# A fused attention and mixer kernel: the token blocks of two pair groups taken whole, and five turns of one group moved from TensorE to DMA

**Chip, cores, metric.** One core of a Trainium2 chip (8 cores on two dies; this program uses one). The metric is the device time of one execution in microseconds (us), the median of several runs.

## The reference

Sigmoid attention for 8 batches x 12 heads (448 tokens, head size 64), then a mixer layer: a token MLP (448 to 256 to 448) on the transposed x, an addition, and a channel MLP (768 to 1536 to 768), another addition.

```python
scores = scale * np.matmul(q, k.transpose(0, 1, 3, 2)) - np.log(S)
attn = 1.0 / (1.0 + np.exp(-scores))
x = np.matmul(attn, v)                      # heads are then laid side by side: (8, 448, 768)
h = np.maximum(x.transpose(0, 2, 1) @ w_tok1, 0.0) @ w_tok2
u = x + h.transpose(0, 2, 1)
h2 = np.maximum(u @ w_ch1, 0.0) @ w_ch2
out = u + h2
```

## The kernel before

Batches 0 and 1 run alone ("A", "B"); batches 2 to 7 are three *pair groups* 1, 2, 3. While the channel matmuls of one group run on TensorE (PE), the attention of the next group is mixed into them, so that ScalarE (ACT), which makes the sigmoids, works beside PE. A Python program plans this: it keeps a rough clock for each engine, and writes the next piece of the main stream (channels) or of the second stream (attention and token MLP) by what is ready. The order on the chip is fixed by that plan. A small edit can therefore reorder everything after it.

One pair of heads gives seven *rounds* of scores (four matmuls and one sigmoid each), then the values, whose result xT has x transposed. The *back* turns it to the tokens' layout. Two ways exist:

```python
def back_by_dma(g, i):                       # one DMA turn on the SP queue
    c = slice(128 * (i % 3), 128 * (i % 3) + 128)
    nc.sync.dma_start_transpose(
        out=x_of(g, i // 3)[:, :, c], in_=xT[(g, i)].rearrange("d b s -> d (b s)")
    )
    did("sp", 1.4, [("xT", g, i)], [("x", g, i)], DMAT)

def back(g, i, at):                          # seven PE transposes and one DVE copy
    ...
    for t in range(J):
        nc.tensor.transpose(out=ps[:, t, :], in_=x[:, 128 * t : 128 * t + 128], identity=ident[:, :])
    nc.vector.tensor_copy(out=x_of(g, i // 3)[:, :, c], in_=ps[:, :, :])
    ...
```

After a group's last pair comes its *token block*: two token matmul groups (first layer, second half) and seven pieces of the second layer. Each of the seven makes u on VectorE (DVE), an fp16 copy u16 on ACT, and a DMA turn of it into uT. All seven turns must land before the group's channel matmuls can start. I call that moment the *hand-over*; there are three, one for each pair group.

```python
u16 = pa.tile([128, D], FP16, tag="attn", bufs=ATTN, name=f"u16_{g}_{t}")   # ATTN = 8
copy("act", u16[:, :], u_of(g, t)[:, :])
...
nc.sync.dma_start_transpose(out=uTs[g][:, :, 128 * t : 128 * t + 128], in_=u16[:, :])
```

The fp16 copies share eight buffers with the sigmoid results. The plan of the second stream, before:

```python
for u, needs, f, made in attention_stays(PAIRS[3:]):   # entries of two rounds each
    if g != u and not late and (g == "B" or out[g][1]):
        g = after_unit[g]
        out[g] = ([], [])
    if late:                                            # the token block: 9 pieces
        out[g][1].append((needs, f))                    # two rounds of the next group first
        take = TAKE[0] if len(late) == 9 else len(late) # TAKE = (5,): 5 pieces, then
        out[g][1].extend(late[:take])                   # two more rounds, then 4 pieces
        late = late[take:]
    else:
        out[g][0].append((needs, f))
    ...
```

Of the kernel before, what the change touches and what calls it, by code (L numbers as in the profile page):

```python
# [21 lines left out]
def kernel(  # L22
# [69 lines left out]
    DIRECT = (3, 0)  # L92
    FROM = (10, 44)
    LATE, MIX = 8, 46
    TAKE = (5,)
    BACK_BY_DMA = [(3, i) for i in range(5)]
    KEYS = ((0, 3), (3, J))
    WARM = 9
    BANKS = ("m0", "m1", "m2", "m3")
# [406 lines left out]
    def tok1(g, half, tcb):  # L506
        x = x_of(g, half)
        ps = pair_bank(f"k1_{g}_{half}_{tcb}", [128, 2, 512])
        for b in range(2):
            for n in range(4):  # L510
                nc.tensor.matmul(  # L511
                    out=ps[:, b, 0:DH],
                    lhsT=w_tok1_of(b, n, tcb),
                    rhs=x[:, n + 3 * b, :],
                    start=(n == 0),
                    stop=(n == 3),
                )
        h = pa.tile([128, 2, DH], FP16, tag="tmp", bufs=4, name=f"h1T_{g}_{half}_{tcb}")
        h1T[(g, half, tcb)] = h
        relu(engine_of(g), h[:, :, :], ps[:, :, 0:DH])  # L520
        pe(1.3, [("x", g, 3 * half + i) for i in range(3)] + [rot["at"]], ["pe"])
        evac(engine_of(g), D, ["pe"], [("h1", g, half, tcb), rot["at"]])
# [8 lines left out]
    def h1_keys(g):  # L531
        if g in SINGLE:
            return [("h1", g, i) for i in range(KD)]
        return [("h1", g, half, t) for half in range(2) for t in range(2)]

    def tok2_pair(g, t):
        ps = pair_bank(f"yn_{g}_{t}", [128, 2, 512])
        for half in range(2):
            for tcb in range(2):
                for b in (0, 1) if t == MIXED else (t // 4,):  # L540
                    c = 64 + 128 * t if t < MIXED else 128 * (t - MIXED)
                    w = w_tok2_of(tcb, c, 128)
                    o = ps[:, half, 0:DH]
                    if t == MIXED:
                        w = w_tok2_of(tcb, S if b == 0 else 64, 64)
                        o = ps[64 * b : 64 * b + 64, half, 0:DH]
                    nc.tensor.matmul(  # L547
                        out=o,
                        lhsT=w,
                        rhs=h1T[(g, half, tcb)][:, b, :],  # L550
                        start=(tcb == 0),
                        stop=(tcb == 1),
                    )
        pe(0.65, h1_keys(g) + [rot["at"]], ["pe"], "col" if t == MIXED else "full")
        for half in range(2):
            dve(0.47, ["pe"], [("u", g, t), rot["at"]])
            nc.vector.tensor_tensor(  # L557
                out=u_of(g, t)[:, DH * half : DH * half + DH],
                in0=x_of(g, half)[:, t, :],
                in1=ps[:, half, 0:DH],  # L560
                op=ADD,
            )
        u16 = pa.tile([128, D], FP16, tag="attn", bufs=ATTN, name=f"u16_{g}_{t}")
        copy("act", u16[:, :], u_of(g, t)[:, :])
        evac("act", D, [("u", g, t)], [("u16", g, t)])
        did("sp", 1.4, [("u16", g, t)], [("uT", g, t)], DMAU)
        state["turned"] = g
        if g not in uTs:
            uTs[g] = pa.tile([128, NDB, 2 * S], FP16, tag="uT", bufs=1, name=f"uT_{g}")
        nc.sync.dma_start_transpose(  # L570
            out=uTs[g][:, :, 128 * t : 128 * t + 128], in_=u16[:, :]
        )

    def tok2_single(g, n, half):

        at = either()
        ps = bank(f"yn_{g}_{n}_{half}", [128, DH], at=at)
        c = 64 - OFF[g] + 128 * n
        for tcb in range(2):
            nc.tensor.matmul(  # L580
                out=ps[:, :],
                lhsT=w_tok2_of(tcb, c, 128),
                rhs=h1T[(g, tcb)][:, half, :],
                start=(tcb == 0),
                stop=(tcb == 1),
            )
        pe(0.33, h1_keys(g) + [f"m{at}"], ["pe"])
        t = n + (3 if g == "B" else 0)
        r = slice(0, 128)
        if t == MIXED:  # L590
            r = slice(0, 64) if g == "A" else slice(64, 128)
        dve(0.47, ["pe"], [("u", g, n), f"m{at}"])
        nc.vector.tensor_tensor(
            out=u_of(g, t)[r, DH * half : DH * half + DH],
            in0=x_of(g, 0)[r, n, half, :],
            in1=ps[r, :],
            op=ADD,
        )
# [516 lines left out]
    def turned_back(g, i):  # L1115

        keys = [("xT", g, i), "m2/m3" if g in SINGLE else "m3"]
        if g not in SINGLE and i % 3 == 0:
            if g == 1:
                keys.append(("u", "AB"[i // 3], 3))  # L1120
            else:
                keys.append(("uT", g - 1, LAST))
        if (g, i) in BACK_BY_DMA:
            del keys[1]
# [14 lines left out]
    def attention_stays(pairs):  # L1139


        out, due, made = [], [], None
        rounds = [(g, i, j) for g, i in pairs for j in range(J)]
        while rounds or due:
            ops, needs, made = [], ["two banks"], None
            if due:
                made = due.pop(0)
                ops.append(lambda at=made: value_stay(*at))
                needs.append(("attn", *made, J - 1))
                needs.append(("one", "value"))  # L1150
                needs += [("x", *ahead(*made, -1))]
            while rounds and len(ops) < 2:
                g, i, j = rounds.pop(0)
                ops.append(lambda at=(g, i, j): one(*at))
                needs += [("k", g, i), ("q", g, i)]
                if j == J - 1:
                    due.append((g, i))
            out.append((g, needs, lambda ops=ops: run(ops), made))
        return out

    def token_entries(g):

        def first(half, t):
            keys = ["one bank"] + [("x", g, 3 * half + i) for i in range(3)]
            return keys, lambda: tok1(g, half, t)

        def second(m):
            keys = [("h1", g, half, t) for half in range(2) for t in range(2)]
            if m >= 5:
                keys.append(("stored", g - 1, STORED[g - 1][m - 5]))  # L1170
            return ["one bank"] + keys, lambda: tok2_pair(g, ORDER[m])

        if g in SINGLE:
            return [], [
                (
                    h1_keys(g) + ["m2/m3", ("x", g, KD - 1)],
                    lambda n=n, half=half: tok2_single(g, n, half),
                )
                for n in range(4)
                for half in range(2)  # L1180
            ]
        return (
            [first(0, 0), first(0, 1)],
            [first(1, 0), first(1, 1)] + [second(m) for m in range(J)],
        )

    def side_stream():

        g, out, late = "B", {"B": ([], [])}, []
        for u, needs, f, made in attention_stays(PAIRS[3:]):  # L1190
            if g != u and not late and (g == "B" or out[g][1]):
                g = after_unit[g]
                out[g] = ([], [])
            if late:
                out[g][1].append((needs, f))
                take = TAKE[0] if len(late) == 9 else len(late)
                out[g][1].extend(late[:take])
                late = late[take:]
            else:
                out[g][0].append((needs, f))  # L1200
            if made and made[0] not in SINGLE and made[1] == NPAIR[made[0]] - 1:
                early, late = token_entries(made[0])
                for n, x in enumerate(early):
                    out[g][0].insert(len(out[g][0]) - 2 + n, x)
        out[g][1].extend(late)
        return out
# [172 lines left out]
    with tc.manual_schedule(engines=None):  # L1379
# [40 lines left out]
        load_pair(1, 1)  # L1420

        stream = side_stream()
        ahead_of_all = [(0.0, *x) for x in stream["B"][0]]
        first_attention(ahead_of_all)
# [144 lines left out]
        for m in range(16):  # L1569
            made = base["B"] + NCB  # L1570
# [42 lines left out]
```

## Time and profile before

| | before |
|---|---|
| median of its first three runs | 373.42 us (373.2 to 374.18) |
| span in the profile | 372.6 us, granted clock 0.988 |
| PE busy | 355.9 us, 96% of the span |
| ACT waits for landed turns (uT) | 7.3 us in 3 waits |
| PE waits for uT at the first hand-over | 2.25 us |

PE is the engine to watch: a change counts if it takes work off PE or closes a hole in it. The lines behind the table are in the prediction.

### The profile page before, as it was taken

To read this page: it belongs to the slowest core of one execution; us is meant where nothing else is said; L and a number is where in the kernel's file an instruction comes from. 1 tells how busy PE (TensorE), PEld (TensorE's weight loads), DVE (VectorE), ACT (ScalarE), POOL (GpSimd) and SP (SyncE) were. 2 spreads that over 40 slices of the span, in tenths; PEclk is the share of its full clock that TensorE was granted. 3 is DMA by queue.
4 is the path that set the end of the run, shared out by engine and by line. 5 is a ranking of instruction groups with operands and counts; after the bars stand their busy time and mean duration, and the time that the engine had idled before them with its cause. 6 is when DMAs were issued, how large, how long until landed. Compare 5 with 4: busy or idle time off the path is not lost.

```text
span 372.6 us, 7828 instructions
## 1 busy us (share of the span) xinstructions
PE 355.9 (96%) x3148; PEld 182.6 (49%) x3148; DVE 235.3 (63%) x440; ACT 195.6 (52%) x240; POOL 132.1 (35%) x213
## 2 busy tenths in 40 slices
PE   6899999999999999799999999899999999999994
PEld 2445545444444555344444555444445556455562
DVE  2267667668645578696643568765644678665862
ACT  2697365666655344367785654287777352243000
POOL 8983313465657510056666410055530000004000
PEclk9699999999999999999999999999999999999998
DMA  6999999889998928798998748798873057400143
GB/s 80 177 193 200 152 211 170 101 147 150 146 149 129 140 49 85 173 164 126 128 121 136 102 103 129 196 164 149 127 122 69 2 126 148 130 0 2 42 147 106
DMA packets 82082, 46.50 MB, mean 125 GB/s; under 512 B 56576, under 2 KB 78336, under 8 KB 82048
## 3 DMA queue, kind: packets, MB, share of 16 engines
q0 software_dynamic: 24576, 21.93, 40.5%
q1 hardware_dynamic: 56912, 22.72, 32.3%
q10 hardware_dynamic: 560, 1.38, 1.0%
q8 instruction: 24, 0.39, 0.4%
q14 instruction: 10, 0.08, 0.1%
HBM read 43.84 MB, written 11.01 MB: 147 GB/s over the span
## 4 chain that ended last, share of the span: by engine, by line
PE 80%; DMA 6%; ACT 6%; DVE 3%; issue 2%; POOL 2%; SPq 0%; ACTq 0%; POOLq 0%
PE x L741 11%; PE qk L422 8%; PE x L1004 7%; PE xa L440 7%; DMA uT<-u 5%; PE z L741 5%; PE k L511 4%; PE c_B L860 4%; PE c_A L860 4%; PE z L1004 3%; PE c_A L918 3%; PE d L1061 3%; PE y L741 2%; PE c_B L918 2%; PE yn L547 2%
## 5 line engine op out<-in xcount | busy, mean ns | idle before, releaser
L429 ACT ACTIVATE attn<-qk 128x896 f16<-128x896 f32 x126 | 109.6, 915 | 50.3 <-PE qk L422 49.9
L741 PEld LDWEIGHTS <-w 128*128 128x128 f16 x378 | 34.3, 98 | 43.1 <-issue 15.1
L422 PE MATMUL qk<-qT,kT 64*64 64x448 f16 x504 | 39.3, 361 | 1.6 <-ACT attn L429 0.8
L741 PE MATMUL x<-uT,w 128*128 128x448 f16 x162 | 37.9, 353 | 2.4 <-DMA uT<-u 2.2
L756 DVE COPY c<-x 128x448 f32<-128x448 f32 x42 | 26.1, 622 | 20.8 <-PE x L741 20.6
L761 DVE CUSTOM_DVE_ANT_0 h2T<-z,c 128x448 f16<-128x448 f32 x36 | 22.5, 624 | 18.5 <-PE z L741 16.3
L394 POOL COPY gate<-kT 1x2 f16<-1x2 f16 x16 | 3.5, 217 | 81.4 <-DMA kT<-pk 81.4
L218 ACT ACTIVATE u<-u 128x768 f16<-128x768 f32 x21 | 17.5, 842 | 24.7 <-DVE u L557 16.9
L246 POOL DMA_DIRECT2D k<-in_k_dram x36 | 21.4, 601 | 23.0 <-PE tk L351 13.2
L1016 DVE TENSOR_TENSOR u<-u,x 128x384 f32<-128x384 f32 x36 | 19.8, 552 | 14.1 <-PE x L1004 14.1
L1004 PEld LDWEIGHTS <-h2T 128*128 128x128 f16 x216 | 20.8, 98 | 15.3 <-issue 2.0
L440 PE MATMUL xa<-attn,v 64*64 64x448 f16 x504 | 27.3, 352 | 0.5 <-ACT attn L429 0.5
L429 ACT ACTIVATE attn_B<-qk_B 128x896 f16<-128x896 f32 x21 | 18.3, 914 | 14.3 <-PE qk_B L422 14.3
L741 PE MATMUL z<-s,w 128*128 128x448 f16 x108 | 24.3, 353 | 0.0
L422 PEld LDWEIGHTS <-kT 64*64 64x64 f16 x504 | 12.4, 104 | 23.0 <-issue 20.6
L557 DVE TENSOR_TENSOR u<-x_nat,yn 128x384 f32<-128x384 f16 x42 | 20.9, 549 | 3.3 <-PE yn L547 2.7
L246 POOL DMA_DIRECT2D v<-in_v_dram x36 | 22.2, 644 | 1.6 <-DMA k<-in_k_dram 1.3
L661 POOL TENSOR_TENSOR r<-h2T,h2T 128x512 f16<-128x512 f16 x1 | 1.2, 1153 | 60.5 <-ACT h2T L230 60.5
L429 ACT ACTIVATE attn_A<-qk_A 128x896 f16<-128x896 f32 x21 | 17.5, 923 | 9.3 <-PE qk_A L422 9.3
L338 POOL COPY pk<-k 128x896 f16<-128x896 f16 x17 | 15.9, 937 | 17.9 <-DMA k<-in_k_dram 17.6
L338 POOL COPY pq<-q 128x896 f16<-128x896 f16 x17 | 15.9, 936 | 17.1 <-DMA q<-in_q_dram 17.1
L246 POOL DMA_DIRECT2D q<-in_q_dram x36 | 21.8, 626 | 0.1
(137 smaller groups left out, 635.9 us busy)
## 6 DMA issues: line engine op xcount, KB each, us to landing
out_dram<-u SPq DMA_DIRECT2D x49, 192.0 KB, 2.9
k<-in_k_dram POOLq DMA_DIRECT2D x36, 112.0 KB, 3.0
q<-in_q_dram POOLq DMA_DIRECT2D x36, 112.0 KB, 4.1
v<-in_v_dram POOLq DMA_DIRECT2D x36, 112.0 KB, 4.3
w<-in_moe_w_ch_dram POOLq DMA_DIRECT2D x2, 1152.0 KB, 11.5
w<-in_moe_w_ch_dram POOLq DMA_DIRECT2D x1, 2304.0 KB, 22.7
out_dram<-u ACTq DMA_DIRECT2D x7, 192.0 KB, 3.2
q_A<-in_q_dram POOLq DMA_DIRECT2D x6, 112.0 KB, 4.4
```

Of the source, the lines that this page charges most:

```text
L246: nc.gpsimd.dma_start(out=t[64 * side : 64 * side + 64, :, :, :], in_=src[b, h + 2 * i : h + 2 * i + 2].rearrange("h (p j) e -> p h j e", ...
L338: nc.gpsimd.tensor_copy(out=m[:, :, :, :], in_=raws[(g, i, what)].rearrange("p h j e -> p j h e"))
L422: nc.tensor.matmul(out=ps[64 * b : 64 * b + 64, h, 0:S], lhsT=keys_of(g, i, j)[r, b, :], rhs=qT[(g, i)][r, :, b, :], start=True, stop=True,)
L429: nc.scalar.activation(out=at[:, :, :], in_=ps[:, :, 0:S], func=SIGMOID, bias=att_bias, scale=att_scale)
L440: nc.tensor.matmul(out=ps[b][64 * h : 64 * h + 64, :], lhsT=vf[r, h, j, :], rhs=attn[(g, i, j)][r, h, :], start=(j == 0), stop=(j == J - 1),)
L557: nc.vector.tensor_tensor(out=u_of(g, t)[:, DH * half : DH * half + DH], in0=x_of(g, half)[:, t, :], in1=ps[:, half, 0:DH], op=ADD,)
L741: nc.tensor.matmul(out=ps[:, :], lhsT=W(p, n, cb), rhs=A[p](n), start=(first and n == 0), skip_group_check=True, stop=(n == KD - 1),)
L756: nc.vector.tensor_copy(out=s[:, :], in_=bk[(cb, "x")][:, :])
L761: nc.vector._custom_dve(dve_ops.TENSOR_ADD_SAT, out=h[half][:, cb, S * b : S * b + S], in0=ps[:, :], in1=snap[(cb, n)][:, :], s0=BIG, s1=0.0,)
L860: nc.tensor.matmul(out=bk[cb][:, :], lhsT=w1[:, n, 128 * cb : 128 * cb + 128], rhs=uTs[g][:, n, OFF[g] : OFF[g] + S], start=(n == 0), stop ...
L1004: nc.tensor.matmul(out=ps[:, :], lhsT=A(p, n, kb), rhs=W(p, kb), start=(first and kb == 0), skip_group_check=True, stop=(kb == KC - 1),)
L1016: nc.vector.tensor_tensor(out=u, in0=u, in1=ps[:, :], op=ADD)
```

## The change

The token blocks of groups 1 and 2 are taken whole (nine pieces) before the next group's fifth and sixth round, so that fewer sigmoid results hold buffers meanwhile; and group 2's first five backs go through DMA as group 3's did already. The sixth back of each group stays on PE.

```diff
-    TAKE = (5,)
-    BACK_BY_DMA = [(3, i) for i in range(5)]
+    TAKE = {1: 9, 2: 9, 3: 9}
+    BACK_BY_DMA = [(g, i) for g in (2, 3) for i in range(5)]
@@ side_stream
-                take = TAKE[0] if len(late) == 9 else len(late)
+                take = TAKE.get(mixed) if len(late) == 9 else len(late)
@@
                 early, late = token_entries(made[0])
+                mixed = made[0]
```

## The prediction

> **What bounds the kernel now.** I read the page first: TensorE (PE) is busy for 96% of the span at almost full granted clock, and the slices show no stage in which it rests, apart from short dips. So a change can only help by taking work off PE or by closing one of those dips.
>
> ```profile
> span 372.6 us, 7828 instructions
> PE 355.9 (96%) x3148; PEld 182.6 (49%) x3148; DVE 235.3 (63%) x440; ACT 195.6 (52%) x240; POOL 132.1 (35%) x213
> ...
> PE   6899999999999999799999999899999999999994
> DMA  6999999889998928798998748798873057400143
> ```
>
> The "7" in the middle of the PE row is the hand-over from the single batches to pair group 1. The DMA row matters too: the 16 engines are 70 to 100% busy for most of the time in which group 2 is prepared (153 to 215 us). Next I took the chain of work that ended last, from 139.8 to 153.5 us. It leaves PE:
>
> ```profile
> 139.61 0.79 PE yn L547 x8
> ...
> 142.39 3.57 DMA uT<-u
> ...
> 146.07 0.76 ACT u L218
> ...
> 148.25 4.32 DMA uT<-u
> 152.56 0.25 issue
> 152.81 0.73 PE x L741 x3
> ```
>
> The token results u are copied to fp16 by ACT, turned by a DMA, and only then can the channel matmuls of the group start. One copy waits for an earlier turn (3.57 us), then a second turn follows (4.32 us). The timelines of ACT and of PE say what this costs:
>
> ```profile
> 146.07 1.64 ACT L218 ACTIVATE u<-u 128x768 f16<-128x768 f32 x2 [2.31 <-DMA uT<-u]
> ```
> ```profile
> 152.81 0.73 PE L741 MATMUL x<-uT,w 128*128 128x448 f16 x3 [2.25 <-DMA uT<-u]
> ```
>
> ACT stood 2.31 us because the fp16 copy had no free buffer, and PE then stood 2.25 us. The program explains the buffer: copies and sigmoid results share eight buffers. While two more rounds of the next group lie inside the block, six sigmoid results are alive and two buffers stay for the last copies. At the hand-over to group 2 the waits from 215 to 241 us are:
>
> ```profile
> ACT u L218 <- DMA uT<-u: 5.0, 2, 3.0
> ...
> PE x L741 <- DVE c L756: 0.8, 1, 0.8
> ...
> PE x L1004 <- DVE u L1016: 0.4, 1, 0.4
> ```
>
> Here ACT stands 5.0 us in two waits, but PE has output matmuls of the old group to do, and loses only 0.8 + 0.4 us.
>
> Last, the turns back. The windows of group 2 show PE full while five of its six turns of x (the backs) run on it:
>
> ```profile
> 180.42 0.73 PE L741 MATMUL x<-s,w 128*128 128x448 f16 x3
> 180.99 0.55 PE L486 MATMUL xb<-ident,xT 128*128 128x128 f16 x7
> 181.47 0.57 PE L422 MATMUL qk<-qT,kT 64*64 64x448 f16 x8
> ```
>
> **What the Trainium skill says.** "Perfetto Trace Analysis", Identifying Performance Opportunities, says that repeated bubbles can mean there is no space for the next tile. The trace agrees, as the three ACT waits on uT (7.3 us in all) show. "VectorE: DVE Perf Modes", The three transpose paths, puts a 128x128 transpose at 390 ns on TensorE and 1309 ns through DMA. So DMA is no faster as such. The trace agrees in direction: the DMA turn of group 3's x takes 4.6 us from issue to landing, seven PE transposes 0.55 us; what is bought is PE time, not latency. "DMA: Bandwidth & Descriptors", Issuing engines are not separate DMA queues, says that all queues end on the same 16 engines and interleave. That is the risk of this change, since the loads of q, k and v run then. The trace has both streams in one window, but one run cannot separate them.
>
> **The change part by part.**
>
> *Backs of group 2.* Five turns of seven transposes leave PE and five copies of 0.62 us leave DVE; five DMA turns of 1.22 us of issue are added to the SP queue. Per back on PE: above, from the start of the three matmuls before it to the scores after it, 181.47 - 180.42 = 1.05 us. Without a back, the same two things stand 0.66 us apart (160.41 to 161.07). So one back costs 0.39 us, five cost 5 x 0.39 = 1.95 us. PE is full there, so this is on the path. DVE is busy 27 to 89% in the ten-microsecond windows from 153 to 203 us and PE hardly waits for it: its 3.1 us count nothing. The added latency has room: the turn lands 4.6 us after issue (6.2 at most in group 3), and the next pair's result, which needs the same buffer, comes 10 us later.
>
> *Block of group 1, hand-over at 152.8.* With all nine pieces ahead of the next rounds, four sigmoid results are alive and four buffers are left for seven copies. The last piece then comes without the scores of two rounds (0.6 us of PE) and without the matmuls that filled the time until their banks were free: about 140 us instead of 142.9. Then two DVE additions (1.0), a copy (0.84) and the queue of seven turns. The first is issued at 136.45, seven at 1.23 each end near 145; with 2.8 to 4.3 us to landing the last lands at 148 to 149.3 instead of 152.6. PE's old work ends near 150.6 - 0.6 = 150.0. So the whole 2.25 us wait should go. The two rounds' 0.6 us are only moved to after the hand-over.
>
> *Block of group 2, hand-over at 237.* The same holds, but PE was covered. The sums on DVE start earlier, so of the 0.8 + 0.4 = 1.15 us at most all goes. The older rounds' 0.6 us move again.
>
> *Group 3.* It has its backs on DMA already and no next group, so its block is as before. It gains two score rounds at its start, moved from group 2's block, and loses nothing; the added 0.6 us balances the 0.6 us that left the first block.
>
> *Sum.* 1.95 + 2.25 + 1.15 = 5.35 us at the very most. I take off about 1.1 us: half of the second hand-over's part, and 0.5 us for new waits, as below. That leaves about 4.2 us: 373.4 - 4.2 = 369.2 us.
>
> **The rivals.**
>
> *The sigmoid stream becomes the bound.* Rounds of scores start 2.31 us apart (161.07, 163.38 and so on), because two banks must be emptied by ACT first. Taking work off PE doesn't speed this stream. Two rounds more at the head of group 2 delay its block by 2.3 us, and the earlier start by about 2.8 us just makes up for that. I reckon group 2's last turn lands near 231.6 us, while PE's old work ends near 231.2 to 231.9: a tie. If the stream is a little slower, a new wait of 1 to 2 us stands at the second hand-over in place of the 1.95 us saved. For it: the eight output pieces left after the block are all the cover there is. Against: group 3's block, already without rounds inside, took 5.9 us from its last token matmul to the last landing, instead of 8.1 (228.32 to 236.45). The time would be 370 to 371.
>
> *DMA contention.* With five more turns, loads and turns of q and k land later. The q turn issued at 186.13 is wanted near 191, so with 3 to 4 us to landing only 1 to 2 us are spare there. For it: DMA share 0.95 to 1.06 between 153 and 180 us, before any turn is added. Against: between 237 and 257 us the same loads with the same five turns ran at a share of 1.0, with PE full from 247 to 267 us. If group 2 doesn't stand it, waits of scores for qT come up, and 1 to 3 us are lost: 370.5 to 372.5.
>
> *Nothing moves at the first hand-over,* because the queue of turns itself is slow, not the buffers: the last turn alone took 4.3 us. Then PE still waits 1 to 2 us, and the time is about 371.
>
> **Range and chances.** The ceiling of the parts is 5.35 us, which gives 368.1; a little more could come if PE's small waits near 197 and 275 us shift well. The rivals give 370 to 372.5. I say 369.2 us, 367.4 to 372.2. Over 2% would need 7.5 us, more than all parts together: 4%. Over 2% slower would need both contention and a badly ordered program, as the order of all instructions is planned anew from this change on: 2%.
>
> **What would show each step right or wrong.** Right: transposes xb on PE fall from 91 to 56, and the DMA turns of x rise from 5 to 10; PE's wait for uT at the first hand-over is gone or under 0.5 us; ACT's waits for uT fall from 7.3 us to under 2; the first channel matmul of group 1 starts near 150 us instead of 152.8, and that of group 2 at 232 to 233 instead of 237.3. The stretch from the last group's hand-over (318 us before) to the end, about 54.5 us, keeps its length. Wrong: PE waits for uT near 232 us (the stream is the bound), PE waits for qT or kT between 155 and 215 us (contention), or x landing over 7 us after issue. If the time is under 367, I have missed a wait that the new order takes away; if it is over 372.5, a new one has come up that none of the above names.

## The result, and the profile after

The changed kernel took 369.5 us (369.23 to 371.04, six runs) against 373.73 us for the kernel before in the same session: ratio 0.9886, 95% interval 0.9846 to 0.9927. In a later session it took 370.42 against 373.75 us: 0.9901 (0.9859 to 0.9943). A ratio is the mean time of one kernel's fast runs over that of the other's of the same rounds, so it is not quite the ratio of the medians. By the 2% rule this is "same"; the gain of about 4 us is clear of the noise.

The page after. PE is busy for the same share of a shorter span, and the "7" of the 17th slice is gone; the DMA row has more nines:

```profile
span 367.5 us, 7770 instructions
PE 351.7 (96%) x3113; PEld 179.4 (49%) x3113; DVE 232.9 (63%) x435; ACT 195.7 (53%) x240; POOL 132.6 (36%) x213
...
PE   6798999999999999999999999899999999999994
DMA  7999999779899838798998996899983158400153
```

The timelines of PE at the first and the second hand-over, after:

```profile
150.14 0.73 PE L741 MATMUL x<-uT,w 128*128 128x448 f16 x3
...
233.76 0.73 PE L741 MATMUL x<-uT,w 128*128 128x448 f16 x3 [1.09 <-DMA uT<-u]
```

The first has no wait any more. The second, which PE reached without a wait before, now has one of 1.09 us; before it was

```profile
237.30 0.73 PE L741 MATMUL x<-uT,w 128*128 128x448 f16 x3
```

ACT's waits over the whole run, and the tile views of the transposes on PE (before, then after) and of the DMA turns of x:

```profile
ACT u L218 <- DMA uT<-u: 2.1, 2, 1.3
```
```profile
L486 PE MATMUL xb<-ident,xT x91: 219/219/230, 75.7 to 295.5; 128*128 128x128 f16 x91
```
```profile
L486 PE MATMUL xb<-ident,xT x56: 218/220/230, 76.1 to 290.3; 128*128 128x128 f16 x56
```
```profile
L463 SPq DMA_TRANSPOSE x_nat<-xT x10: 1221/1251/1423, 157.7 to 277.4; - x10
...
DMA to landing us min/median/max: 2.9/5.2/9.0
```

ACT's wait fell from 7.3 to 2.1 us, 35 transposes left PE (91 to 56), and the turns of x now take up to 9.0 us to land. PE's slot where a back stood is closed; from the three matmuls to the scores it is 0.66 us, where it was 1.05:

```profile
181.32 0.73 PE L741 MATMUL x<-uT,w 128*128 128x448 f16 x3
181.98 0.57 PE L422 MATMUL qk<-qT,kT 64*64 64x448 f16 x8
```

**A finer clock than the total.** Total times of one kernel scatter by several us (372.97 to 378.36 in one session of the kernel before), and two profiles of the change, whose spans differ by 2.8 us, are 3.1 us apart before anything that the change touches. So I cut every profile at four moments of PE: the first second-layer token matmul of group 1 (yn; up to it the change's program is that of the kernel before, on every engine), and the first channel matmul of groups 1, 2 and 3 (the hand-overs). Each column below is the difference between two such starts, the last one up to the end of the span. The kernel names are those of the experiments; all these profiles are in the fast state.

| kernel | yn to 1st hand-over | 1st to 2nd | 2nd to 3rd | 3rd to end | sum |
|---|---|---|---|---|---|
| before | 19.19 | 84.49 | 80.77 | 54.53 | 238.98 |
| before, again (b1) | 17.71 | 84.64 | 80.75 | 54.57 | 237.67 |
| change | 16.15 | 83.62 | 79.06 | 54.68 | 233.51 |
| change, again (a1) | 16.15 | 83.31 | 79.06 | 54.65 | 233.17 |
| blocks only (e1, again) | 16.15 | 83.98 | 80.77 | 54.76 | 235.66 |
| backs only (e2) | 17.54 | 82.63 | 79.83 | 54.36 | 234.36 |
| before + buffers (e3, again) | 16.77 | 83.97 | 80.31 | 54.53 | 235.58 |
| first block only (e4) | 16.15 | 87.94 | 79.04 | 54.52 | 237.65 |
| change + buffers (e5) | 16.15 | 83.37 | 79.06 | 54.35 | 232.93 |
| block before more rounds (e6) | 16.49 | 84.26 | 80.50 | 54.37 | 235.62 |
| group 1's backs too (e8) | 16.15 | 84.15 | 80.70 | 54.47 | 235.47 |
| turns doubled (e9) | 16.15 | 86.73 | 79.06 | 54.21 | 236.15 |

The same program repeats to 0.3 us in each stretch, with one exception: the first stretch of the kernel before. So the change saves 2.3 + 1.1 + 1.7 - 0.1 = 5.0 us after yn, as the means of two profiles each; the medians of the total times say 3.3 to 4.2 us.

The stretches don't hold the same work in every kernel, as the plan moves rounds across the hand-overs. The score matmuls (qk) of the first three are 8, 168 and 144 in the kernel before, and 0, 184 and 136 in the change (four make a round). So the change's second stretch holds four rounds more, about 1.3 us of PE, two from each side; its third holds two fewer, 0.6 us. Where before one pair of rounds stood inside group 2's block, the change has two pairs behind the block, both ahead of the hand-over (before, then after):

```profile
222.15 0.63 PE L422 MATMUL qk<-qT,kT 64*64 64x448 f16 x8
```
```profile
228.55 0.57 PE L422 MATMUL qk<-qT,kT 64*64 64x448 f16 x8
...
232.09 0.57 PE L422 MATMUL qk<-qT,kT 64*64 64x448 f16 x8
```

The sum of the stretches is free of this; a comparison of single stretches needs the same counts.

### The profile page after: what moved, and what is told of

Same layout as the page of the kernel before. It is cut to its first block, busy times and chain, and to the rows that moved or that the text cites. A ratio compares the mean times of both kernels' runs of the same rounds, so it can differ in the third digit from the quotient of the medians.

```text
span 367.5 us, 7770 instructions
## 1 busy us (share of the span) xinstructions
PE 351.7 (96%) x3113; PEld 179.4 (49%) x3113; DVE 232.9 (63%) x435; ACT 195.7 (53%) x240; POOL 132.6 (36%) x213
## 4 chain that ended last, share of the span: by engine, by line
PE 79%; DMA 7%; POOL 4%; DVE 4%; ACT 3%; issue 2%; ACTq 0%; POOLq 0%
PE x L741 11%; PE x L1004 8%; PE qk L422 7%; PE xa L440 6%; PE z L741 5%; PE c_B L918 4%; PE k L511 4%; PE z L1004 4%; PE c_A L860 4%; PE c_B L860 4%; PE c_A L918 3%; PE d L1061 3%; DMA w<-in_moe_w_ch_dram 3%; PE yn L547 3%; PE y L741 2%; PE y L1004 2%
## 5 line engine op out<-in xcount | busy, mean ns | idle before, releaser
L429 ACT ACTIVATE attn_A<-qk_A 128x896 f16<-128x896 f32 x21 | 17.5, 924 | 8.0 <-PE qk_A L422 8.0
```

Of the source, the lines that this page charges most:

```text
L429: nc.scalar.activation(out=at[:, :, :], in_=ps[:, :, 0:S], func=SIGMOID, bias=att_bias, scale=att_scale)
```

## The experiments

**The kernel before and the change once more (b1_before_again, a1_after_again).** No edit. How much of a profile is a draw?

> The kernel before against itself, for a second profile and as a measure of noise. The stretches between landmarks in PE's timeline were the same to 0.4 us in two profiles of the change (first token matmul of group 1 to first hand-over 16.15 and 16.15; first to second hand-over 83.62 and 83.31; second to third 79.06 and 79.06). If the 2.25 us wait at the first hand-over of the kernel before is a draw, its first stretch will be between 17.5 and 19.2 us here, the second 84.5 and the third 80.8 within 0.3 us. Ratio 1.00.

> The changed kernel once more, beside the next three, for their comparison and for a second profile. If the 2.25 us wait for uT that the kernel before showed at its first hand-over was partly a draw of DMA landing times (the same instructions in e2_backs_only waited 0.6 us), the waits at the hand-overs of the change should be a draw too: first hand-over 0 to 0.5 us, second 0.5 to 1.5 us. Time 4 us under before.

Measured: b1 374.25 us, ratio to itself 1.0019 (0.9977 to 1.0060), which is the noise of all the ratios here; a1 0.9901. PE at the first hand-over of b1, and at the second of a1:

```profile
151.84 0.73 PE L741 MATMUL x<-uT,w 128*128 128x448 f16 x3 [0.78 <-DMA uT<-u]
```
```profile
236.59 0.54 PE L741 MATMUL x<-uT,w 128*128 128x448 f16 x2 [1.04 <-DMA uT<-u]
```

The wait on which the prediction put 2.25 us was 0.78 us here, and 0.60 us in e2, whose program is the same up to that point on every engine. The chain in e2 shows the last turn landing 2.83 us after its issue, where the first profile had 4.32. So the wait at the first hand-over is a draw of landing times, of 0.6 to 2.25 us in three profiles. The wait at the second hand-over of the change, in contrast, repeats (1.09, 1.04).

**Each half alone (e1, e2).** Only one of the two edits each:

```diff
 e1:  -    BACK_BY_DMA = [(g, i) for g in (2, 3) for i in range(5)]
      +    BACK_BY_DMA = [(3, i) for i in range(5)]
 e2:  TAKE as before, BACK_BY_DMA as in the change
```

> The blocks of groups 1 and 2 whole as in the change, but group 2's backs stay on PE. My theory (two separate gains, both in PE time): the first hand-over comes about 3.0 us earlier as in the change (near 150 us, no wait for uT), the second keeps its cover because PE still has 5 x 0.39 us of transposes, so the 1.1 us wait of the change at the second hand-over is under 0.3 us. Time 3 us under before: 370.7 us, that is about 1 us over the change. Rival 1 (the sigmoid stream bounds group 2, the backs gave nothing): the same time as the change, 369.5. Rival 2 (the added DMA turns cost by contention): faster than the change, under 369.

> The blocks of groups 1 and 2 whole, group 2's backs on PE; again, since the first profile was in the slow state. Theory (the backs' PE time is what hid the second hand-over's turns): first stretch 16.15 us, no PE wait for uT at the second hand-over or under 0.3 us, second stretch longer than the change's by 1.95 less the 1.05 us wait, that is by 0.9 us: about 84.4 us; third about 79.1. Rival (the wait of 1.05 us there is due to the queue of turns whatever PE does): second stretch longer by the whole 1.95 us and the wait stays at about 1 us.

> Group 2's backs through DMA, the blocks split 5 and 4 as before. Theory: PE loses 5 x 0.39 = 1.95 us of work between the first and second hand-over; the first hand-over stays at 152.8 with its 2.2 us wait for uT; at the second, where the two rounds inside the block keep the last turns late, part of it comes back as a wait for uT of 0.5 to 2 us. Time 0.3 to 1.5 us under before, 372.5. Rival (all saved PE time counts): 371.7 or less with no wait at the second hand-over. Rival (contention): slower than before.

Measured: the blocks alone 0.9932 (0.9883 to 0.9981) in one session, where the profile fell in a slow state (granted clock 0.75) and is not used, and 0.9895 (0.9866 to 0.9923) in another; the backs alone 0.9911 (0.9856 to 0.9965), 370.53 us. Total times cannot split the change: each half's interval overlaps that of the whole. The stretches can. From yn to the end, against the mean of the two profiles before, e1 saves 2.7 us, e2 4.0 us (0.9 of it the draw in the first stretch) and the change 5.0 us: less than both halves together.

*The backs.* In e2 the stretch from first to second hand-over is 82.63 us against 84.57 (mean of the two profiles before): 1.94 us less, with the same number of matmuls otherwise. The prediction's 5 x 0.39 = 1.95 us is met. My theory for e2, that part of it would come back as a wait for uT of 0.5 to 2 us at the second hand-over, failed: no such wait shows there, and the rival (all saved PE time counts) holds.

*The tie.* In e1, PE still has group 2's transposes, and reaches the second hand-over without a wait:

```profile
233.67 0.74 PE L741 MATMUL x<-uT,w 128*128 128x448 f16 x3
```

e1 and the change hold the same rounds and values in this stretch, and differ by the backs. So the change should be 1.94 us shorter; it is 83.98 - 83.47 = 0.5 us shorter, and 1.07 us of the missing 1.4 is the new wait. This is the first rival of the prediction, in the size that it gave (1 to 2 us): with less to do, PE arrives before the last turn. (The expectation of 84.4 us for this stretch of e1 was 0.4 us too long.)

*The third stretch.* About 79.1 us was expected for e1, and this missed: it has 80.77, with the change's number of matmuls and 1.3 us of waits of scores for ACT that the change hasn't. I don't know their cause; both orders are planned anew.

**Buffers, without touching the block (e3), and on top of the change (e5).** The sixth and seventh fp16 copy go to the raw k and q buffers, which are idle then:

```diff
-        u16 = pa.tile([128, D], FP16, tag="attn", bufs=ATTN, name=f"u16_{g}_{t}")
+        tag, bufs = {ORDER[5]: ("rk", 1), ORDER[6]: ("rq", 1)}.get(t, ("attn", ATTN))
+        u16 = pa.tile([128, D], FP16, tag=tag, bufs=bufs, name=f"u16_{g}_{t}")
```

(Ten shared buffers in place of eight would have been simpler, but they didn't fit: 155.4 kB per partition asked, 152.0 left. Told by the build, nothing ran.)

> The kernel before with nothing changed but the buffers of the sixth and seventh fp16 copy of u of each pair group: they take the idle raw k and q buffers and not the shared eight. Theory (the first hand-over's wait comes from the lack of free buffers): ACT's 2.31 us wait for uT goes, the last turn is issued about 2 us earlier, PE's wait for uT at the first hand-over falls from 2.2 to under 0.7 us; time 1.5 to 2.2 us under before, 371.7. Rival (the queue of turns itself is slow): ACT's wait goes but PE's wait stays over 1.5 us and the time stays within 0.5 us of before.

> The kernel before with two more buffers for the fp16 copies, again since the first profile was in the slow state. Theory (buffers delay the last turns): the first stretch falls to about 17 us, that is 16.15 plus the two rounds of 0.6 us, with no wait for uT on PE; second stretch 84.5 or up to 0.8 us less; Rival (the queue of turns is slow by itself): PE still waits 0.6 us or more for uT at the first hand-over.

> The change with the sixth and seventh fp16 copy of u in the idle raw k and q buffers. Theory (at the second hand-over the copies' waits of 0.78 and 1.28 us for free buffers lie on the chain of the last turn, and PE's wait of 1.09 us there is what is left of it): ACT's waits for uT go from 2.1 us to 0, the second hand-over comes about 1 us earlier without a PE wait; 0.5 to 1.2 us under the change. Rival (the turns' queue is the chain): ACT's waits go, PE's wait stays, same time as the change.

e3: 0.9946 (0.9900 to 0.9992), its first profile slow and not used; again 0.9968 (0.9932 to 1.0004). The last copies at the first hand-over, ACT's timeline of e3, where before they began at 146.07 after a wait for uT:

```profile
143.61 1.77 ACT L218 ACTIVATE u<-u 128x768 f16<-128x768 f32 x2 [0.55 <-DVE u L557]
145.94 0.84 ACT L218 ACTIVATE u<-u 128x768 f16<-128x768 f32 x1 [0.55 <-DVE u L557]
```

They wait only for u itself now, PE has no wait at the hand-over, and the stretch is 16.77 us, which is the change's 16.15 plus the 0.6 us of the two rounds still inside. So the lack of buffers was the cause at the first hand-over. Its worth, against the 17.5 to 19.2 us of the unedited block, is 0.8 to 2.4 us.

e5: 0.9871 (0.9837 to 0.9905), 369.08 us, the fastest median of all. But its stretches are the change's to within 0.3 us, so I don't claim a faster version; its median leads a1's by 1.3 us, and the two profiles differ mostly ahead of yn (133.27 against 137.13 us). ACT's waits for uT fell from 2.1 to 1.0 us, not to 0 as expected. PE's wait at the second hand-over stayed:

```profile
232.79 0.54 PE L742 MATMUL x<-uT,w 128*128 128x448 f16 x2 [1.09 <-DMA uT<-u]
```

ACT's three last copies now ended 2.0 us before the last turn was issued; they run from 225.85 on, and the turns are issued one behind the other:

```profile
225.85 2.38 ACT L218 ACTIVATE u<-u 128x768 f16<-128x768 f32 x3 [1.00 <-DMA uT<-u]
```
```profile
228.89 2.57 SPq L571 DMA_TRANSPOSE uT<-u  x2
230.22 1.24 SPq L571 DMA_TRANSPOSE uT<-u  x1
```

(The first of the two SP lines holds the turn issued at 228.89 and that of 230.22.) The last five turns start 1.33 us after one another, and the queue has no gap from the second turn on. So at the second hand-over the queue of turns, not the buffers, sets the last landing: my theory for e5 failed and its rival holds.

**The first block only (e4).** `TAKE = {1: 9, 2: 5, 3: 5}`, backs as before.

> Only the block of group 1 whole, that of group 2 split as before, backs of group 2 on PE. Theory: the first hand-over about 3 us earlier; the two rounds moved behind it cost 0.6 us of PE there, so 2.3 us under before: 371.2. The second block's part is then e1_block_only less this, 0.3 to 1 us. Rival (the order of the whole changes by more than the block, gains come from elsewhere): the first hand-over moves less than 2 us, or this is as fast as e1_block_only.

Measured 373.64 us, 0.9984 (0.9941 to 1.0027): of the 2.3 us expected, no gain clear of the noise is left. The theory failed, and neither of the rival's two signs came. The first hand-over did come early (16.15 us), but the next stretch took 87.94 us. PE just ahead of the second hand-over:

```profile
235.75 1.52 PE L440 MATMUL xa<-attn,v 64*64 64x448 f16 x28 [1.98 <-ACT attn L429]
```

The replanned order put a values piece and five more rounds ahead of the hand-over (28 and 20 matmuls more than before), behind a block that is still split; the values waited for a sigmoid, which waited 1.50 us for a turn to land to get its buffer. Of the 3.4 us added, PE's busy time accounts for 2.6 (85.6 us instead of 83.0; the third stretch gives 1.7 back) and the wait for 2.0, while some 1.0 us of other waits went. So under this plan the first block pays only if the second is taken whole as well.

**The block even earlier (e6).** The block goes ahead of the next group's third and fourth round too (`out[g][1].extend(late)` first, the rounds into the next group's list).

> The change, with each block taken even before the next group's third and fourth round (one more entry of the sigmoid stream moved behind it). Theory (the sigmoid stream sets when the block can start): the block starts up to 2.3 us earlier, six buffers are free for the copies, PE's wait at the second hand-over is gone: 0.5 to 1.2 us under the change, but the stream itself falls behind by one entry in each group, so it may come back at the next hand-over; in that case the same time. Rival (PE work is the bound, the wait of 1.09 us was a draw): within 0.3 us of the change.

Measured 371.31 us, 0.9933 (0.9900 to 0.9966), about 1 us over a1. ACT waits for uT nowhere any more, yet PE waits 0.74 us for uT at the second hand-over, and at the third, where the change had none:

```profile
315.03 0.54 PE L741 MATMUL x<-uT,w 128*128 128x448 f16 x2 [1.14 <-issue]
```

(The profile names no releaser here, but the last turn of u landed at 314.94.) The block of group 2 didn't start earlier, as the theory had it: its first yn stands 70.2 us after the first hand-over, where the change has 69.2, and 1.3 us of waits of scores for ACT are new in between. That the sigmoid stream falls behind by its moved entry would explain this, but it is not shown. As it stands, this goes too far.

**More turns by DMA (e8), and the same turns twice (e9).** e8: `BACK_BY_DMA` for groups 1, 2 and 3. e9: in `back_by_dma`, for group 2, the same `dma_start_transpose` is issued a second time into the same place.

> The change, with group 1's first five backs through DMA too. Theory: another 5 x 0.37 = 1.9 us of PE work goes between 75 and 125 us, and the stream is not near the hand-over there, so 1 to 1.9 us under the change. Rival (contention: the weights of the channels and the loads of v, k and q are under way there, the DMA share is 0.9 to 1.0): turns of x land over 8 us after issue, PE waits for k or q, same or slower than the change.

> The change with every DMA turn of group 2's x issued twice, into the same place, so the suspected contention of these turns is doubled and PE's work unchanged. Theory (the loads have room enough): second stretch within 0.3 us of 83.3 to 83.6, waits of PE for qT or kT between the first and second hand-over under 0.5 us in sum, same time as the change within 0.5 us. Rival (contention is already at the edge): PE waits for qT, kT or v appear, 1 us or more longer.

e8: 372.57 us, 0.9960 (0.9929 to 0.9991), 2 us over a1. Ahead of 135 us, PE now waits for q, as the rival said (its other sign, turns of x landing over 8 us after issue, didn't come: 6.9 at most), and the two waits eat what the five backs save:

```profile
PE qk L422 <- DMA qT<-pq: 2.4, 2, 2.1
```

Stretches two and three are 0.7 and 1.6 us over the change's as well. The second has a wait of scores for ACT of 1.3 us that the change hasn't. The third holds the same matmuls, but the granted clock fell. The page's clock rows, of the change and of e8:

```profile
PEclk9999999999999999999999999999999999999998
```
```profile
PEclk9999999999899999999999999899999999999998
```

The two "8" inside the second row are stretches of 3.4 us at a clock of 0.50, from 99.28 and from 235.81 us; each costs PE about 1.7 us by my estimate (half of 3.4), and the second is the whole 1.6 us. Both begin within 0.2 us of the end of a wait of PE (2.1 us for q; 1.3 us for ACT and 0.4 us for uT). That the waits brought them is not shown: the kernel before waited 2.25 us at its first hand-over and kept a clock of 1.00.

e9: 374.26 us, 0.9991 (0.9954 to 1.0027): the whole gain is gone. The stretch with the doubled turns is 86.73 us, 3.3 over the change's. I had expected that the loads have room, and for q and k that is so (0.2 us of PE waits for qT in all). The damage came in by another door. The waits of ACT and of PE in this stretch:

```profile
ACT xT L218 <- DMA x_nat<-xT: 7.2, 3, 3.8
```
```profile
PE qk L422 <- ACT xT L218: 1.5, 1, 1.5
PE qk L422 <- ACT attn L429: 1.3, 3, 0.4
```

xT has one buffer. ACT cannot write the next pair's xT before the turn of the last has read it; behind ACT's xT stand the sigmoids, behind these the scores. In the change itself no ACT wait of this kind shows.

But this run doesn't double the traffic, as I had meant it to. The second turn writes the same place, and the SP queue issues it only when the first has landed (at 163.63 after 158.19, at 174.76 after 169.47, and so on). The queue's own waits:

```profile
SPq L467 <- DMA x_nat<-xT: 19.7, 5, 5.5
```

So a doubled turn holds xT for 9.1 to 10.8 us from the first issue to the second landing, where the change's turn takes 2.9 to 9.0, and it holds the SP queue, with all that stands behind it, for 4.1 to 8.1 us in place of 1.2. The run shows what a longer hold costs; which of the two holds costs how much isn't separated, and contention of twice as many turns at once stays untested.

## Why the prediction was right

The time was forecast at 369.2 us and came out at 369.5, in the middle of the range 367.4 to 372.2. Step by step:

- *Five backs on PE, 1.95 us.* Right: 1.94 us by e2. That DVE's 3.1 us count nothing also fits, as e2's stretch needs no more than PE's share.
- *First hand-over, 2.25 us of wait and a start near 150.0.* The mechanism is right: with whole blocks the group's channel matmuls start at 150.14, without a wait, and e3 shows that buffers were the cause. The size was a draw: three profiles of the same instructions give waits of 2.25, 0.78 and 0.60 us. Against the mean of the two profiles of the kernel before, the stretch falls by 2.3 us, of which 0.6 us are rounds moved on. (The prediction's sum for the last turn counted its landing from the end of its issue, which gave 148 to 149.3; the trace counts from the start, and the turn issued at 144.85 landed at 147.65.)
- *Second hand-over, at most 1.15 us.* The waits named are gone at this hand-over (0.8 us for c, in the third stretch, and 0.4 us for u, in the second; 0.2 us for c is new behind the first hand-over). With them went 0.6 us of small waits of scores in each of the two stretches, which the sum hadn't.
- *The moved rounds.* This step failed. The prediction moved two rounds from group 2's block to behind the second hand-over, so that the third stretch would grow by 0.6 us. They stayed ahead of it, and two more came (168 to 184 score matmuls in the second stretch, 144 to 136 in the third). So the third stretch became 1.7 us shorter: 0.6 by rounds that the second took over, 1.1 by closed waits. Against that, the first two stretches saved 3.4 us where the parts, with rounds and deduction, had about 4.9. That these two misses (some 1.5 us too much in the one, 2.3 too little in the other) largely cancel is luck.
- *A tie at the second hand-over as a rival.* It came: 1.04 to 1.09 us, in both profiles. Group 2's block also started late, as this rival said: at 219.30 us, where it was 218.16 before, though the first hand-over came 2.7 us earlier. So the deduction of 1.1 us, made for "new waits" and half of the second hand-over's share, was right in sum because the wait took 1.07 us while the other small waits gave some back: luck again.
- *Contention as a rival.* It came in the landing times, and cost PE nothing. The loads of q in the second stretch, before and after:

```profile
q<-in_q_dram POOLq DMA_DIRECT2D x12, 112.0 KB, 4.2
```
```profile
q<-in_q_dram POOLq DMA_DIRECT2D x12, 112.0 KB, 6.3
```

  Their median is 4.0 to 4.4 us in the profiles without group 2's turns on DMA (before, b1, e1), and 5.1 to 6.3 us with them (change, a1, e2). The turns of q, which were to land later too, did not (2.9 to 3.2 us in before and b1, 2.9 in the change and a1), and PE waits for neither qT nor kT in this stretch. One of the tests that I named, x landing over 7 us after issue, was a wrong test: turns took up to 9.0 us and PE lost nothing. e9 shows a better one: ACT's wait for the turn before it rewrites xT. The prediction had this buffer in its account, with 10 us until the next pair's result; e9's holds of 9.1 to 10.8 us are where waits appear.
- *ACT's waits for uT under 2 us.* 2.1 and 2.0 us, a near miss; they are all at the second hand-over, where e5 halved them and PE's wait stayed. The second hand-over came at 233.76, not at 232 to 233: the tie again.

What stays open: the 0.8 to 1.7 us between the gain after yn in the profiles (5.0 us) and the 3.3 to 4.2 us of the medians. The stretch ahead of yn, which the change leaves alone, varied from 133.3 to 137.1 us in these profiles, enough to hide it.

## What to carry to other kernels

Cut profiles at fixed moments and compare stretch by stretch: here totals that scatter by several us hid parts that repeat to 0.3 us. Count the work in each stretch first, and look at its clock. One profile's wait for a DMA can be three times the next one's. Two savings on both sides of one meeting point don't add up: taking 1.9 us of work off the engine that was to cover a chain of transfers turned 1.1 us of it into a wait on that chain. Before moving work to DMA, look at which single buffer the transfer holds and for how long: here a turn of up to 9.0 us cost PE nothing, and holds of 9.1 to 10.8 us, which also blocked the queue, cost 3.3 us.

## What the Trainium skill lacked or had wrong

- "VectorE: DVE Perf Modes", The three transpose paths, gives 390 ns on TensorE against 1309 ns by DMA for one 128x128 block. It has no figure for a run of blocks. Here seven PE transposes cost PE 0.39 us in all (1.94 us for 35), and one DMA turn of the whole 128x896 tile 2.9 to 9.0 us from issue to landing, with 1.2 us on the issuing queue.
- "DMA: Bandwidth & Descriptors", Issuing engines are not separate DMA queues, says that all queues share 16 engines, but no page gives the spread of landing times of a DMA turn: the last turn of u landed 2.83 and 4.32 us after issue in two profiles (e2 and before) of a program that is the same up to there, and PE's wait behind it was 0.60 to 2.25 us.
- No page gives the spacing of DMA turns of this size queued on one issuing queue: the last five turns of u started 1.33 us apart, each with 1.24 us on the queue, and this, not the buffers, set the second hand-over (e5).
- "Perfetto Trace Analysis", Identifying Performance Opportunities, speaks of bubbles on the engine that should be saturated. Here the shortage of buffers (e3) showed on another engine: ACT stood 5.0 us for uT at the second hand-over before, and PE, the busy engine, had no wait for uT there.
